# A recurrence and a two-layer block on one core: SyncE left out of the path for large h, and the last block's output turned by TensorE and stored in two transfers

## The chip, the cores and the metric

The kernel runs on 1 core of one Trainium2 chip. The metric is the time of one execution in device microseconds (us), the median over several runs. The span of a trace, from its first to its last instruction, is about 1.8 us shorter than the time of the same run.

In the views of the profile PE is TensorE, PEld its loading of weights, DVE VectorE, ACT ScalarE, POOL GpSimd and SP SyncE; a q behind the name is the engine's sequencer, the part that waits, branches and issues transfers, and L521 is line 521 of the kernel. A semaphore is a counter by which engines and transfers tell each other that they are done. An instruction fetch is a transfer that brings an engine its next instructions; the traces list these as packets of kind "instruction".

## The reference

```python
# attention part: B, S, D = 4, 6080, 256
sig = 1.0 / (1.0 + np.exp(-f_logit))
f = lower_bound + (1.0 - lower_bound) * sig
i = 1.0 - f
for t in range(S):
    h = f[:, t] * h + i[:, t] * x[:, t]
    y[:, t] = h
# second part, on all 24320 tokens: w_in 256 x 2048, w_out 2048 x 256
h = x @ w_in
g = h - np.tanh(h)
out = g @ w_out
```

The output is 24320 rows of 256 numbers in float32, 1 KB a row.

## The kernel before

The tokens are handled in 48 blocks: one of 256 and 47 of 512. A short polynomial stands for `h - tanh(h)` as long as all h are small. A flag watches that, and at the very end every engine reads the flag and branches: if some h was large, `general()` does all the work again with the real tanh. With these inputs that path is never run, but its code lies in the program, between the branch and the end.

In the main path a block's result stands in a tile `C` with channels on partitions. It has to be turned before it is stored with tokens as rows. VectorE turns it in squares of 32 x 32, which leaves rows of 64 numbers (256 B) on the partitions, and SyncE stores it with one transfer for each group of 32 partitions. The last block does this in four pieces and in two halves:

```python
def turn_out(j, slots=None):
    ...
    for slot in slots or (None,):
        ...
        nc.vector.transpose(out=dst[:, js, k], in_=src[:, js, k])

def send(j, half=None):
    ...
    dst = out[starts[j] : starts[j] + sizes[j], :].rearrange(
        "(j b) (i c) -> i b j c", b=H, i=G
    )
    for i in range(G):                      # G = 4: rows of 64 numbers
        nc.sync.dma_start(
            out=dst[i][:, js], in_=acc[j, "out"][i * H : (i + 1) * H, js])

def end(j):                                 # the last block alone
    ...
    for half, slot, r in ((0, 2, 1), (1, 1, 0)):
        nc.vector.tensor_tensor(
            out=C[:, slot], in0=acc[j, 3][:, r, 0:hb], in1=C[:, slot], op=ALU.add)
        turn_out(j, (slot,))
        send(j, half)
```

The last steps in the order of the program, and the branch:

```python
if (name, j) == ("o1", NBLK - 1):
    tc.mark_branch_hint_location("general", "LikelyTaken")
    nc.vector.reduce_max(out=worst[:], in_=flags[:], axis=mybir.AxisListType.X)
if j == NBLK - 1 and name in ("o4", "otr"):
    if name == "o4":
        sum_up()        # two tiny matmuls and a copy: worst -> flag
        end(j)
    continue
steps[name](j)
if (name, j) == ("o3", NBLK - 1):
    turn_out(j, (0, 3))
...
fast()
seen = nc.values_load(flag[:].bitcast(INT32), ...)   # on all five engines
with tc.If(seen != 0, label="general"):
    general()           # all its transfers are issued by nc.sync
```

## Time and profile before

| | before |
|---|---|
| median time | 2337.45 us (three runs, 2335.92 to 2338.53) |
| span of the trace | 2334.70 us |
| TensorE busy | 2318.4 us (99%) |
| start of the reduction of the flags to the end | 16.95 us |
| last arithmetic to the end | 11.45 us |

The prediction below shows the views that carry the argument. Two more are of use. First, who SyncE waited for at the end (engine and line waiting, what ended the wait, us in total, times, longest):

```profile
SPq L1006 <- SPq L1006: 2.4, 1, 2.4
```

A wait of an engine for its own branch is the time of a far jump, a branch over all of `general()` to the end: SyncE had nothing else to wait for. Second, the view of the output tile in the last 12.7 us (line, engine, operation, tiles and count; duration in ns as min/median/max; first and last start), with the time from issue to landing below it:

```profile
L521 SPq DMA_DIRECT2D out_dram<-osb x8: 315/450/2198, 2322.5 to 2329.3; - x8
...
DMA to landing us min/median/max: 1.9/3.6/3.8
```

Most issues take 0.45 us, but the longest took 2.2, and a store of 64 KB takes 1.9 us at best and 3.6 in the middle.

### The profile page before, as it was taken

The page shows a single profiled execution, that of the slowest core. Times are in us where ns is not written, and L with a number is a line of the kernel's source. Part 1 is how long each engine was busy: PE and PEld are TensorE (multiplying, and loading weights), DVE is VectorE, ACT ScalarE, POOL GpSimd, SP SyncE. Part 2 cuts the span into 40 slices and gives each one's busy share as a digit, 9 for nine tenths or more (in the row PEclk, how much of TensorE's full clock was granted, in tenths as well). Part 3 has the DMA queues.
Part 4 walks back from the last instruction along what each step waited for, and adds up shares of the span by engine and source line. Part 5 has one row for each costly group of instructions (what it writes and reads, how often), then busy time and mean ns, then how long its engine had stood idle before and what let it go on. Part 6 is the DMA issues. An engine that isn't in the chain of part 4 may idle for free.

```text
span 2334.7 us, 28635 instructions
## 1 busy us (share of the span) xinstructions
PE 2318.4 (99%) x10669; PEld 2024.6 (87%) x10669; DVE 2121.2 (91%) x2450; ACT 1800.4 (77%) x2685; POOL 0.7 (0%) x6
## 2 busy tenths in 40 slices
PE   9999999999999999999999999999999999999997
PEld 6888888888888888888888888888888888888886
DVE  8999899998999999998999989999899998999987
ACT  7677777777777777777777777777777777778774
POOL 0000000000000000000000000000000000000000
PEclk9999999999999999999999999999999999999999
DMA  5211111111111211112111121111211111111101
GB/s 172 63 23 35 39 37 28 28 39 35 37 28 28 45 29 37 28 28 46 31 34 28 28 46 36 28 28 30 44 37 28 28 36 37 37 28 28 28 10 29
DMA packets 298564, 85.05 MB, mean 36 GB/s; under 512 B 292016, under 2 KB 294320, under 8 KB 298416
## 3 DMA queue, kind: packets, MB, share of 16 engines
q1 hardware_dynamic: 298272, 83.14, 16.9%
q8 instruction: 85, 1.39, 0.3%
q14 instruction: 63, 0.52, 0.1%
q10 hardware_dynamic: 144, 0.00, 0.0%
HBM read 58.20 MB, written 24.90 MB: 36 GB/s over the span
## 4 chain that ended last, share of the span: by engine, by line
PE 99%; DMA 0%; SPq 0%; DVE 0%; issue 0%; DVEq 0%
PE A L383 27%; PE Qa L466 14%; PE Qb L466 14%; PE D L383 14%; PE Qd L466 14%; PE Qc L466 7%; PE B L383 7%; PE Qc L745 1%; PE Qa L745 1%; PE Qb L745 1%; PE A L678 1%; PE D L678 0%; PE Qd L678 0%; DMA xn<-in_x_dram 0%; PE B L678 0%; PE Qc L678 0%
## 5 line engine op out<-in xcount | busy, mean ns | idle before, releaser
L383 PE MATMUL A<-T,w_in 128*128 128x256 f32 x2208 | 558.8, 379 | 0.0
L383 PEld LDWEIGHTS A<-T,w_in 128*128 128x128 f32 x2208 | 419.5, 190 | 57.0
L427 DVE TENSOR_TENSOR h<-h,q 128x1024 f32<-128x1024 f32 x368 | 437.3, 1219 | 3.1
L421 DVE SCALAR_TENSOR_TENSOR q<-q,t 128x1024 f32<-128x1024 f32 x368 | 439.8, 1215 | 0.0
L414 ACT ACTIVATE q<-t 128x1024 f32<-128x1024 f32 x368 | 382.9, 1053 | 46.3 <-DVE h L427 43.4
L411 ACT ACTIVATE t<-h 128x1024 f32<-128x1024 f32 x368 | 388.6, 1056 | 3.1 <-DVE h L398 0.3
L432 ACT ACTIVATE junk<-t 128x1024 bf16<-128x1024 f32 x368 | 388.2, 1055 | 1.5
L446 DVE TENSOR_TENSOR Tg<-h 128x1024 f32<-128x1024 f32 x368 | 347.8, 945 | 6.3
L466 PE MATMUL Qb<-h,w_out 128*128 128x256 f32 x1472 | 347.7, 379 | 0.0
L466 PEld LDWEIGHTS Qb<-h,w_out 128*128 128x128 f32 x1472 | 279.7, 190 | 38.0
L466 PE MATMUL Qa<-Tg,w_out 128*128 128x256 f32 x736 | 219.0, 379 | 0.0
L466 PE MATMUL Qd<-Tg,w_out 128*128 128x256 f32 x736 | 218.9, 379 | 0.0
L466 PE MATMUL Qd<-h,w_out 128*128 128x256 f32 x736 | 218.9, 379 | 0.0
L466 PE MATMUL Qa<-h,w_out 128*128 128x256 f32 x736 | 218.9, 379 | 0.0
L395 ACT COPY h<-B 128x512 f32<-128x512 f32 x184 | 107.0, 581 | 143.3 <-PE B L383 94.5
L395 ACT COPY h<-A 128x512 f32<-128x512 f32 x184 | 107.2, 583 | 136.7 <-PE A L383 125.3
L398 DVE TENSOR_TENSOR h<-D,r 128x512 f32<-128x512 f32 x184 | 126.8, 689 | 93.6 <-PE D L383 91.3
L398 DVE TENSOR_TENSOR h<-A,r 128x512 f32<-128x512 f32 x184 | 126.2, 686 | 74.6 <-PE A L383 42.5
L395 ACT COPY r<-A 128x512 f32<-128x512 f32 x184 | 107.2, 583 | 106.0 <-PE A L383 106.0
L383 PE MATMUL B<-y,w_in 128*128 128x256 f32 x736 | 188.9, 379 | 0.0
L383 PE MATMUL D<-y,w_in 128*128 128x256 f32 x736 | 188.9, 379 | 0.0
L383 PE MATMUL A<-y,w_in 128*128 128x256 f32 x736 | 188.9, 379 | 0.0
(114 smaller groups left out, 3068.3 us busy)
## 6 DMA issues: line engine op xcount, KB each, us to landing
xn<-in_x_dram SPq DMA_DIRECT2D x184, 128.0 KB, 3.3
fn<-in_f_logit_dram SPq DMA_DIRECT2D x184, 128.0 KB, 3.2
out_dram<-osb SPq DMA_DIRECT2D x180, 128.0 KB, 2.8
raw<-in_moe_w_in_dram SPq DMA_DIRECT2D x8, 512.0 KB, 5.2
raw<-in_moe_w_out_dram SPq DMA_DIRECT2D x8, 512.0 KB, 4.7
fn<-in_f_logit_dram SPq DMA_DIRECT2D x1, 512.0 KB, 6.6
xn<-in_x_dram SPq DMA_DIRECT2D x1, 512.0 KB, 7.4
out_dram<-osb SPq DMA_DIRECT2D x1, 512.0 KB, 2.9
```

What stands on the lines that cost most here:

```text
L383: nc.tensor.matmul(ps[:, c], lhsT=w_in[u][:, slot, c * P : (c + 1) * P], rhs=mixes[j][right], start=start and c == 0, stop=True, skip_grou ...
L395: nc.scalar.copy(out=dst, in_=piece(n, bank))
L398: nc.vector.tensor_tensor(out=piece(n, "h")[:, q], in0=piece(n, bank), in1=piece(n, r), op=ALU.add)
L411: nc.scalar.activation(out=half(n, i, "t"), in_=half(n, i), func=AF.Square)
L414: nc.scalar.activation(out=half(n, i, "q"), in_=half(n, i, "t"), func=AF.Square, scale=RA, bias=RB,)
L421: nc.vector.scalar_tensor_tensor(out=q, in0=q, scalar=RC, in1=t, op0=ALU.add, op1=ALU.mult)
L427: nc.vector.tensor_tensor(out=h, in0=h, in1=q, op=ALU.mult)
L432: nc.scalar.activation(out=junk[:, :, :, 0 : st[n]["hb"]], in_=t, func=AF.Relu, bias=-TINY, accum_out=flags[:, 2 * n + i : 2 * n + i + 1],)
L446: nc.vector.tensor_tensor(out=o, in0=a, in1=b, op=ALU.subtract)
L466: nc.tensor.matmul(acc[j, part][:, r, 0 : st[n]["hb"]], lhsT=w_out[u][:, slot, c * P : (c + 1) * P], rhs=piece(n, right)[:, q, c], start=( ...
L678: nc.tensor.matmul(h[c], lhsT=w_in[u][:, 2 * k + s, c * P : (c + 1) * P], rhs=ys[j][:, k, 0:nb], start=k == 0 and (c == 0 or len(banks) == 2),
L745: nc.tensor.matmul(acc[j][i // 2][:, i % 2].rearrange("p (k m) -> p k m", k=2), lhsT=plain[j, u][:, s, c, i * P : (i + 1) * P], rhs=w_out[ ...
```

## The change

Two things are changed. The transfers of the path for large h are issued by GpSimd, so that SyncE has no code there to jump over. And the last block is turned by TensorE, 128 x 128 at a time, evicted by ScalarE (first half) and VectorE (second half), and stored in rows of 1 KB, one transfer of 256 KB for each half. Beside that, the flag is made earlier and a branch hint goes. The diff, cut to its core:

```diff
-        def fetch(j, parts=(0, 1)):
+        def fetch(j, parts=(0, 1), queue=nc.sync):
...
-                    nc.sync.dma_start(
+                    queue.dma_start(
...
         def end(j):
             hb = sizes[j] // 2
             C = acc[j, "C"][:, 0 : 4 * hb].rearrange("p (n t) -> p n t", n=4)
-            for half, slot, r in ((0, 2, 1), (1, 1, 0)):
+            osb = opool.tile([P, NQ, D], FP32, name="osb", tag="osb")
+            for half in range(2):
+                slot, r = ((2, 1), (1, 0))[half]
                 nc.vector.tensor_tensor(
                     out=C[:, slot], in0=acc[j, 3][:, r, 0:hb], in1=C[:, slot], op=ALU.add
                 )
-                turn_out(j, (slot,))
-                send(j, half)
+                name = ("Qa", "Qb")[half]
+                bank = ps_b.tile([P, 2, KC, P], FP32, name=name, tag=name)
+                for i in range(2):
+                    for k in range(KC):
+                        nc.tensor.transpose(
+                            bank[:, i, k], C[:, 2 * k + half, i * P : (i + 1) * P], ident[:]
+                        )
+                rows = osb[:, 2 * half : 2 * half + 2]
+                (nc.scalar.copy, nc.vector.tensor_copy)[half](
+                    out=rows.rearrange("p i (m k) -> p i k m", k=KC), in_=bank[:]
+                )
+                t0 = starts[j] + half * hb
+                nc.sync.dma_start(
+                    out=out[t0 : t0 + hb, :].rearrange("(i p) d -> p i d", p=P), in_=rows
+                )
...
-                            tc.mark_branch_hint_location("general", "LikelyTaken")
...
-                                sum_up()
                                 end(j)
                             continue
+                        if (name, j) == ("o3", NBLK - 1):
+                            sum_up()
                         steps[name](j)
-                        if (name, j) == ("o3", NBLK - 1):
-                            turn_out(j, (0, 3))
...     # in general(): weights, inputs and output
-                    fetch_w(u, raw[:], nc.sync)
+                    fetch_w(u, raw[:], nc.gpsimd)
-                fetch(j)
+                fetch(j, queue=nc.gpsimd)
-                nc.sync.dma_start(
+                nc.gpsimd.dma_start(
...
-    with tc.If(seen != 0, label="general"):
+    with tc.If(seen != 0):
```

More of the change, by code (lines that the diff above doesn't have):

```diff
@@ L498, in finish, with give @@
             nc.vector.tensor_tensor(out=o, in0=a, in1=b, op=ALU.add)
-        def turn_out(j, slots=None):
+        def give(j):
             n = sizes[j] // H
-            if (j, "out") not in acc:
-                acc[j, "out"] = opool.tile([P, TB // H, H * KC], FP32, name="osb", tag="osb")
-            dst = acc[j, "out"][:, 0:n].rearrange("p j (a k) -> p j k a", k=KC)
-            src = acc[j, "C"][:, 0 : n * KC * H].rearrange(
-                "p (k j b) -> p j k b", k=KC, b=H
-            )
-            for slot in slots or (None,):
-                k, s = (slice(None), 0) if slot is None else (slot // 2, slot % 2)
-                js = slice(0, n) if slot is None else slice(s * n // 2, (s + 1) * n // 2)
-                nc.vector.transpose(out=dst[:, js, k], in_=src[:, js, k])
-        def send(j, half=None):
-            n = sizes[j] // H
-            js = slice(0, n) if half is None else slice(half * n // 2, (half + 1) * n // 2)
+            osb = opool.tile([P, TB // H, H * KC], FP32, name="osb", tag="osb")
+            nc.vector.transpose(
+                out=osb[:, 0:n].rearrange("p j (a k) -> p j k a", k=KC),
+                in_=acc[j, "C"][:, 0 : n * KC * H].rearrange(
+                    "p (k j b) -> p j k b", k=KC, b=H
+                ),
+            )
             dst = out[starts[j] : starts[j] + sizes[j], :].rearrange(
@@ L521, in send @@
                 nc.sync.dma_start(
-                    out=dst[i][:, js],
-                    in_=acc[j, "out"][i * H : (i + 1) * H, js],
-                )
-        def give(j):
-            turn_out(j)
-            send(j)
+                    out=dst[i],
+                    in_=osb[i * H : (i + 1) * H, 0:n],
+                )
         def end(j):
```

## The prediction

> **What bounds the kernel now.** I read the page first (engines, then the chain that ended last), then the end of the chain in order of time, then the views of the three lines that come after the last arithmetic. The page of the kernel before, engines and chain:
>
> ```profile
> PE 2318.4 (99%) x10669; PEld 2024.6 (87%) x10669; DVE 2121.2 (91%) x2450; ACT 1800.4 (77%) x2685; POOL 0.7 (0%) x6
> ...
> PE 99%; DMA 0%; SPq 0%; DVE 0%; issue 0%; DVEq 0%
> ```
>
> TensorE is busy 2318.4 of 2334.7 us and the chain is TensorE: the body is bound by matmuls. The diff touches nothing in it (the stores of the 45 blocks before the last stay one VectorE transpose and four transfers each), so all it can win lies in the 16 us that TensorE is not busy, nearly all at the end. The chain of the last microseconds (start, length, what):
>
> ```profile
> 2318.92 0.88 PE Qc L466 x4
> 2319.80 0.02 issue
> 2319.82 0.43 DVE C L498
> ...
> 2320.89 0.77 DVE osb L512 x2
> 2321.66 0.33 DVE C L535
> 2321.99 0.02 issue
> 2322.01 0.45 DVE osb L512
> 2322.45 0.32 DVE C L535
> 2322.78 0.02 issue
> 2322.80 0.45 DVE osb L512
> ```
>
> Arithmetic ends at 2323.25, but the span at 2334.70: 11.45 us follow in which no engine computes. The timeline of SyncE (start, length) and the view of the line of the branch (duration ns, first and last start) say what they are:
>
> ```profile
> 2322.48 7.24 SPq L521 DMA_DIRECT2D out_dram<-osb  x8
> ```
>
> ```profile
> L1006 SPq EVENT_SEMAPHORE  x8: 17/17/17, 2332.8 to 2333.3; - x8
> ...
> L1006 POOLq COMPARE_BRANCH  x1: 45/45/45, 2322.4 to 2322.4; - x1
> L1006 PEldq COMPARE_BRANCH  x1: 4127/4127/4127, 2322.4 to 2322.4; - x1
> L1006 DVEq COMPARE_BRANCH  x1: 72/72/72, 2323.4 to 2323.4; - x1
> L1006 ACTq EVENT_SEMAPHORE  x1: 17/17/17, 2325.2 to 2325.2; - x1
> L1006 DVEq EVENT_SEMAPHORE  x1: 21/21/21, 2326.5 to 2326.5; - x1
> L1006 PEldq EVENT_SEMAPHORE  x1: 51/51/51, 2326.6 to 2326.6; - x1
> L1006 SPq COMPARE_BRANCH  x1: 45/45/45, 2330.3 to 2330.3; - x1
> ```
>
> SyncE is the last of all. From the single records (to the ns): eight issues 2322.48 to 2329.72 (six of 0.32 to 0.46 us, two of 2.20 and 2.14 us); read of the flag 2329.78 to 2330.27; branch at 2330.34; first instruction beyond it at 2332.82, **2.48 us** later; eight semaphore adds (0.59 us to the first wait of the end); eight waits and a drain to 2333.97; closing barrier to 2334.70 (**0.73 us**). The last packet of the output had ended at 2330.75, so no landing bounds this end: SyncE's own code does. GpSimd, which has no code in the path for large h, passes its branch and drains 0.16 us later (2322.40, 2322.56). Every engine with code there needs far more: ScalarE 2.85 us, VectorE 3.08, TensorE 4.18, SyncE 2.48. Each has an instruction page fetched 0.9 to 1.0 us after its branch. Both 2.2 us issues enclose a 16 KB instruction fetch of TensorE's (packets at 2323.47, 1.64 us, and 2327.31, 1.53 us); between the opening (its first 17 us) and the end there are ten more issues over 0.9 us, and all ten lie on such a fetch. So a store issued during TensorE's fetch is held about 2 us.
>
> **What the Trainium skill says.** (1) "Runtime: NRT & Kernel Launch", section Instruction fetch mechanics: a taken branch whose target isn't in the window held forces a fetch before execution can go on. The trace agrees: 2.5 to 4.2 us for the four engines that jump far, 0.16 us for the one that doesn't. (2) "DMA: Bandwidth & Descriptors", Specifications: line rate wants at least 512 B a descriptor; and Anatomy of one DMA: about 2 us are fixed, mostly the write receipt. The trace: rows of 256 B, 64 KB, took 3.6 us to land (median of eight); a store of 256 KB in rows of 1 KB took 2.2 us. Four times the data in less time agrees on both. (3) "VectorE: DVE Perf Modes", Why PSUM operands drop a tier: 1x only for fp32 from PSUM, so 512 columns at 0.96 GHz are 0.53 us plus overhead; the adds of 512 columns out of PSUM here took 0.69 us, which I use.
>
> **The change part by part.** *Flag earlier.* The two tiny matmuls for the flag go between Qc and Qd on TensorE. Before, they started 0.1 us behind the matmul rhythm and are 0.08 us loads: I put 0.2 us on Qd, whose end goes from 2321.51 to 2321.71. ScalarE copies the flag at about 2320.1 instead of 2321.67; this is off the path.
> *VectorE.* The four transposes of 256 columns (0.77 + 0.45 + 0.45 us of chain) go. The two adds (0.39 us each) start when Qd lands: 2321.8 to 2322.2 and 2322.2 to 2322.55. Before, the first waited for the transposes until 2321.58, so here little is won: the adds end 0.2 us earlier than 2322.77.
> *TensorE transposes.* In the opening the same operation has this record (min/median/max ns):
>
> ```profile
> L623 PE MATMUL Qb<-ident,fn x6: 283/283/417, 6.6 to 11.0; 128*128 128x128 f32 x6
> ```
>
> Two passes each, 0.12 us apart: 0.24 us a transpose. The first half's first needs no add and hides; three follow the add: 2322.25 to 2322.85, + 0.28 us of the last pass = 2323.13. The second half's four: last pass at 2323.81, end 2324.09.
> *Evictions.* ScalarE: 512 columns took 0.58 us (line 395), a start 0.1 us after the last pass: 2323.23 to 2323.82. VectorE: 2324.19 to 2324.88 (0.69).
> *Stores.* The same form of store stands in the opening:
>
> ```profile
> L762 SPq DMA_DIRECT2D out_dram<-osb x2: 400/402/404, 111.2 to 121.2; - x2
> ```
>
> Two issues of 0.40 us instead of eight: 2323.85 and 2324.9 to 2325.3. Landed 2.2 us after the issue starts, as its fastest did: 2327.1. SyncE then reads the flag (0.49 us), passes the branch as GpSimd did before (0.16 us) and waits for the landing; its eight adds go to GpSimd. A drain at about 2327.5. So **SyncE is 6.5 us earlier**, and it is no longer last.
> *The jump of the others.* Now the bound is the jump that starts last. TensorE reads the flag behind its last transpose, 2323.9; read and branch took 0.585 us (2321.856 to 2322.441), the jump 4.18, the drain 0.15: 2328.9. VectorE reads it when its eviction has started, 2324.2; + 0.62 + 3.08 + 0.11 = 2328.0. ScalarE 2323.25 + 0.53 + 2.85 + 0.09 = 2326.7. GpSimd now jumps too, but its flag comes at 2320.2; with TensorE's full 4.18 us and ten adds it is done by 2326.
> *Sum.* Last drain 2328.9 (TensorE), + 0.73 us barrier = 2329.65; before 2334.70. Gain **5.05 us**, 0.22%. The branch hint that goes is taken as worth nothing: with it, all four far jumps still fetched after their branch. GpSimd's transfers stand in the path not run: nothing in the body.
>
> **Rivals.** (a) *The second store is caught by TensorE's fetch.* Fetch at branch + 1.03 us = 2325.5; the issue ends by my sum at 2325.3, 0.2 us before. If it slips, it is held some 2 us: landing about 2328.9, drain 2329.2, end 2330.0. Costs only 0.3 us, since TensorE's jump is as long. For it: both issues that met such a fetch were held. About 1 in 3.
> (b) *The bound passes to GpSimd's or TensorE's jump, longer than measured*, as the hint is gone or as pages collide: GpSimd's jump has no record. 1 to 2 us more: 2333.5 to 2334.5. The early flag speaks against GpSimd.
> (c) *All is hidden*: were the output's landing the end, removing code would win nothing. Against it: the last packet ended 3.95 us before the end.
> (d) *A new cost in the body or the start* (other page borders, transfers on GpSimd's queue set up at the launch). I see nothing in the profile for it; at most a microsecond.
>
> **Range and chances.** 2337.45 - 5.05 = **2332.4 us**. The three runs before spread over 2335.92 to 2338.53, so the median alone is good to about 1.2 us; rivals (a) and (b) add up to 1.5 above, and shorter jumps up to 1 below. Range 2330.5 to 2334.6. 2% would be 47 us; the whole idle tail is 11.45 us, so neither more than 2% faster nor slower can come from here: 0.98 within 2%, 0.01 each way.
>
> **What would show it.** Right: SyncE's record at the branch is short and no adds follow it; two issues of 0.4 us in place of 7.24 us; the last to drain is TensorE, 4 us after a branch near 2324.5; the span is 2329 to 2331. Wrong: TensorE busy more than 0.2% longer in the body; a second store of over 2 us of issue (rival a); GpSimd last to drain (rival b); the span's end set by the landing; adds or far jump still on SyncE.

## The result, and the profile after

| | before | after |
|---|---|---|
| median time | 2336.56 us (six runs, 2335.92 to 2338.53) | 2331.41 us (six runs, 2330.55 to 2332.59) |
| span of the trace | 2334.70 us | 2329.32 us |
| start to the first product of the third block | 85.22 us | 85.49 us |
| from there to the reduction of the flags | 2232.54 us | 2232.54 us |
| reduction of the flags to the end | 16.95 us | 11.28 us |

The ratio of the times is 0.9977, with a 95% interval of 0.9964 to 0.999. A ratio is the mean time of one kernel's runs over that of the other's of the same rounds, so not quite the ratio of the medians quoted. The change is 5.2 us faster by the medians, and 5.38 us by the spans.

The last three rows cut the span in three. The middle is the same to 0.01 us in every trace, fourteen in all. The opening, where loads of inputs and weights meet, lasts from 85.2 to 87.4 us from trace to trace, whatever the kernel. That is most of the 2 us by which runs of one kernel differ, so the medians can't tell apart versions of the end that differ by a microsecond. The trace can: from here on, **"the end" is the time from the start of the reduction of the flags to the end of the span.** It is 5.67 us shorter after the change.

The chain that ended last, in the changed kernel (start, length, what; it follows arithmetic alone and stops at the last eviction):

```profile
2319.20 0.86 PE Qc L466 x4
2320.06 0.12 PE most L840 x2
2320.18 1.94 PE Qd L466 x8
...
2322.14 0.43 DVE C L526
...
2322.62 0.55 PE Qa L533 x3
2323.17 0.52 PE Qb L533 x4
...
2323.71 0.69 DVE osb L537
```

The arithmetic now ends 1.15 us later than before in the span, at 2324.40 in place of 2323.25 (0.28 us of that is the opening). The gain is not there. It lies behind it, in the view of the line of the branch:

```profile
L1009 POOLq EVENT_SEMAPHORE  x4: 17/43/43, 2324.0 to 2324.2; - x4
L1009 POOLq COMPARE_BRANCH  x1: 45/45/45, 2321.3 to 2321.3; - x1
L1009 PEldq COMPARE_BRANCH  x1: 3711/3711/3711, 2323.7 to 2323.7; - x1
...
L1009 DVEq COMPARE_BRANCH  x1: 72/72/72, 2324.3 to 2324.3; - x1
L1009 SPq COMPARE_BRANCH  x1: 50/50/50, 2325.6 to 2325.6; - x1
L1009 ACTq EVENT_SEMAPHORE  x1: 17/17/17, 2326.5 to 2326.5; - x1
L1009 PEldq EVENT_SEMAPHORE  x1: 51/51/51, 2327.4 to 2327.4; - x1
L1009 DVEq EVENT_SEMAPHORE  x1: 21/21/21, 2327.6 to 2327.6; - x1
```

SyncE branches at 2325.6 and no longer has semaphore adds behind its branch; its next instruction starts 0.19 us later. GpSimd has them instead, 2.7 us after its own branch at 2321.3. All jumps are over at 2327.6. Yet the span ends at 2329.32. What SyncE waits for, and how long the two stores take:

```profile
SPq L1039 <- DMA out_dram<-osb: 1.9, 2, 1.4
```

```profile
L541 SPq DMA_DIRECT2D out_dram<-osb x2: 389/389/389, 2323.8 to 2324.4; - x2
...
DMA to landing us min/median/max: 3.7/3.7/3.8
```

Two short issues replace the eight, but each store takes 3.7 us to land, and SyncE waits for that. The last landing is at 2328.18, SyncE drains at 2328.51, and the closing barrier takes 0.81 us. So **the landing of the last store sets the new end**, not a jump.

The single records say why it takes so long. A store runs on 16 DMA engines and each posts its own part of the semaphore; the Trainium skill ("DMA: Bandwidth & Descriptors", Why a DMA increments its semaphore by 16 and not by 1) describes this, and the trace has 16 updates for each store. For the second store, issued at 2324.43, eleven of the 16 arrive between 2326.54 and 2326.70, the next four by 2327.56, and the last at 2328.18. A packet of 16 KB, an instruction fetch of TensorE's after its branch, lies from 2324.71 to 2325.96, and smaller ones of 8 KB from 2324.60 on. The same page (Queues, rings and completion order) says that a DMA engine drains a whole packet of one queue before it turns to another. That fits: a part of the store that shares an engine with the fetch has to wait. It was an idea at this point; the experiments test it.

### The profile page after: what moved, and what is told of

The parts are those of the page before. It is cut to its first block, busy times and chain, and to the rows that moved or that the text cites. A ratio compares the mean times of both kernels' runs of the same rounds, so it can differ in the third digit from the quotient of the medians.

```text
span 2329.3 us, 28648 instructions
## 1 busy us (share of the span) xinstructions
PE 2319.6 (100%) x10677; PEld 2025.2 (87%) x10677; DVE 2121.4 (91%) x2447; ACT 1801.1 (77%) x2686; POOL 0.7 (0%) x6
## 4 chain that ended last, share of the span: by engine, by line
PE 99%; DMA 0%; SPq 0%; DVE 0%; issue 0%
PE A L383 27%; PE Qd L466 14%; PE Qa L466 14%; PE Qb L466 14%; PE D L383 14%; PE Qc L466 7%; PE B L383 7%; PE Qc L749 1%; PE Qb L749 1%; PE Qa L749 1%; PE A L682 1%; PE D L682 0%; PE Qd L682 0%; DMA xn<-in_x_dram 0%; PE B L682 0%; PE Qc L682 0%
```

## The experiments

My theory after the result: before the change, the end was SyncE's own code, that is eight issues of which two were held by TensorE's instruction fetch, then a jump of 2.5 us, then adds. The new end wins by getting its stores issued ahead of the fetch, and what is left of it is the landing of the last store, held by instruction fetches. The rivals: SyncE's jump is the whole gain; TensorE's transposes are the gain in themselves; two stores of 256 KB so close together need 3.7 us anyway; a branch costs the same, fetch or no fetch.

All of the runs gave right results on these inputs. The ends, in one table:

| run | what it is | the end, us | last store, issue to landing, us |
|---|---|---|---|
| before | | 16.95 | 1.9 |
| sp_free | before, SyncE out of the path for large h | 13.69 | 2.4 |
| no_branch_before | before, no path for large h at all | 11.06 | 1.9 |
| after | | 11.28 | 3.75 |
| after_again | the same | 12.02 | 4.49 |
| end_only | after, SyncE back in the path | 12.00 | 3.72 |
| eight_stores | after, eight stores of 64 KB | 15.69 | 1.7 |
| flag_late | after, flag made behind Qd | 10.73 and 10.76 | 3.5 |
| no_branch_after | after, no path for large h at all | 9.76 | 2.35 |
| near_jump | after, path for large h cut to some 20 to 40 instructions | 11.72 | 4.21 |
| near_jump_shift | the same, page border moved | 9.86 | 2.35 |
| pe_waits | after, TensorE's jump made 3.9 us later | 14.53 | 3.09 |
| pe_lingers | after, idle matmuls behind the transposes | 11.16 | 3.62 |

### SyncE's part alone

The end stays as before; `fetch`, `fetch_w` and the output of `general()` go to GpSimd:

```diff
 # before.py, general()
-                    fetch_w(u, raw[:], nc.sync)
+                    fetch_w(u, raw[:], nc.gpsimd)
...
-                fetch(j)
+                fetch(j, queue=nc.gpsimd)
...
-                nc.sync.dma_start(
+                nc.gpsimd.dma_start(
```

> The kernel before with one part of the change: the transfers of the path for large h are issued by GpSimd, the end is unchanged (VectorE transposes, eight stores of 64 KB). My theory, from the trace of before (span 2334.7 us): the eight issues still run until about 2329.7, two of them held 2 us each by TensorE's instruction fetch; then SyncE reads the flag and passes its branch in 0.2 us, so the jump of 2.5 us and the eight adds of 0.6 us go; now the last store's landing, 2331.1 in the trace of before, ends it: end = 2331.1 + 0.3 (last waits) + 0.75 (barrier) = 2332.2, that is 2.5 us less than before. Rival 1, SyncE's code is the whole of the change's gain: 5.4 us less. Rival 2, SyncE's code is hidden behind something else: 0.

Measured: the end went from 16.95 to 13.69 us, 3.26 less (ratio of the times 0.9992, interval 0.9978 to 1.0005, so the times alone don't show it). The jump and the adds are gone, and SyncE now waits for the landing:

```profile
SPq L1036 <- DMA out_dram<-osb: 0.2, 1, 0.2
```

It is 0.8 us more than my theory's 2.5, and the last issue ended 0.93 us earlier after the end of Qd: TensorE's two fetches were shorter in this trace (1.16 and 0.96 us in place of 1.64 and 1.53). The rival that asked for 5.4 us falls, and so does the one that asked for nothing.

### The new end alone

```diff
 # after.py, general(): all three back to nc.sync
-                    fetch_w(u, raw[:], nc.gpsimd)
+                    fetch_w(u, raw[:], nc.sync)
...
-                fetch(j, queue=nc.gpsimd)
+                fetch(j, queue=nc.sync)
...
-                nc.gpsimd.dma_start(
+                nc.sync.dma_start(
```

> The changed kernel with the other part undone: SyncE issues the transfers of the path for large h again, the end is the new one. My theory: the second issue ends at 2324.8 as in the changed kernel, flag read and branch at 2325.6, jump 2.5 us, adds 0.6, waits 0.55, barrier 0.75: end near 2330.0, 4.7 us less than before and 0.7 more than the changed kernel. The two parts alone would then sum to 7.2 us, more than the 5.4 of both together, as each shortens the same chain. Rival, the gains add: 5.4 - 2.5 = 2.9 us less than before.

Measured: 12.00 us, 4.95 less than before (ratio 0.998, 0.9967 to 0.9994). SyncE is back at its jump:

```profile
SPq L1009 <- SPq L1009: 2.5, 1, 2.5
```

The two parts alone sum to 3.26 + 4.95 = 8.2 us and together gave 5.67, as my theory said: they shorten the same chain. The new end is the larger part. Given the new end, taking SyncE out is worth 12.00 - 11.28 = 0.7 us against the first trace of the changed kernel and nothing against its second (12.02), as then the landing takes over.

### No branch at all

`values_load`, `tc.If` and `general()` are deleted from either kernel. These kernels are right for small h alone and serve as a measurement.

> The changed kernel without the path for large h and without its branch (right for these inputs alone). My theory: in the changed kernel the last store lands 3.7 us after its issue because one DMA engine carries TensorE's 16 KB instruction fetch first (15 of the 16 engines had posted within 3.1 us, eleven within 2.3); without a jump there is no fetch, the second store lands 2.2 us after its issue, near 2326.6, and the span ends near 2327.7: 1.6 us less than the changed kernel, 7.0 less than before. Rival, two stores of 256 KB so close together need 3.7 us anyway: landing 2328.2 and the span 2329.0 to 2329.3.

> The kernel before without the path for large h and without its branch (right for these inputs alone). My theory: no issue is held any more, eight issues of 0.45 us take 3.7 instead of 7.2 us, 2322.5 to 2326.2; last landing near 2327.5, span near 2328.6: 6.1 us less than before, and only 0.9 us above the changed end without a branch. So nearly all that the new end wins, it wins by getting its stores issued ahead of TensorE's fetch. Rival, the new end is itself much faster (transposes, wide rows): 2332 or more, 4 us above no_branch_after.

Measured for the changed kernel: 9.76 us. All 16 parts of the last store post within 0.20 us, and it lands 2.35 us after its issue. The view of the output tile:

```profile
DMA to landing us min/median/max: 2.2/2.3/2.3
```

So two stores of 256 KB that close together need 2.3 us, not 3.7; that rival falls. For the kernel before, 11.06 us, and no issue is held:

```profile
L521 SPq DMA_DIRECT2D out_dram<-osb x8: 316/459/467, 2323.7 to 2327.1; - x8
```

Without a branch the new end is 11.06 - 9.76 = 1.3 us better than the old one (I had put 0.9). With the branch and SyncE free it is 13.69 - 11.28 = 2.4 us better, or 1.7 against the second trace. So once SyncE is free, at most 1.1 us of what the new end wins, less than half, can come from its two issues being ahead of the fetch; the other 1.3 us are there without any fetch. My "nearly all" was wrong there. It fits better with SyncE in the path of both, where each hold of an issue also delays SyncE's jump: of 16.95 - 12.00 = 4.95 us only 1.3 are there without a fetch. The trace of before has the fetch 1.96 us after the end of Qd, and the third of eight issues ran into it; in the changed kernel the second and last issue began 0.28 us before the fetch and was not held (0.39 us). The times of both show no more than the medians allow (0.9977 and 0.9981).

### Jump or fetch

The path for large h is cut to one quarter of one block, so that the target of the branch is near. The kernel would be wrong for large h.

```diff
 # after.py, general()
-            for u in range(NU):                    # weights
+            for u in range(1):
...
-            for j, nb in enumerate(sizes):
+            for j, nb in enumerate(sizes[:1]):
...
-                for u in range(NU):                # products
+                for u in range(1):
...
```

> The changed kernel with the path for large h cut down to one quarter of one block, some 20 to 40 instructions an engine in place of 709 to 4,629 (it would be wrong for large h, which these inputs never have; the branch, the flag and the end stay). Measured in the trace from the start of the reduction of the flags to the end of the span: before 16.95 us, changed 11.28, changed without the branch 9.76. My theory, it is the far jump's instruction fetch that costs, not the branch: no 16 KB fetch after the branch, TensorE drains within 0.5 us of its branch, the last store lands 2.3 to 2.5 us after its issue, 9.8 to 10.1 us. Rival, a taken branch costs the same near or far: 11.3.

Measured: 11.72 us, which neither side had. TensorE's branch is short:

```profile
L1009 PEldq COMPARE_BRANCH  x1: 367/367/367, 2325.3 to 2325.3; - x1
```

but the stores are slower than ever:

```profile
DMA to landing us min/median/max: 4.2/4.2/4.2
```

The records show the cause: one 16 KB packet of TensorE's queue still came, 1.1 us after its branch, and it took 1.73 us. Fifteen parts of the last store posted within 0.17 us, the sixteenth 1.9 us after them. In the traces TensorE's fetches come 218 to 288 of its records apart, 256 on average (without the first of a trace and those behind the branch), so I take one fetch to bring a page of some 256 instructions (an estimate from these distances). The last fetch before this one was 274 records earlier: the program happened to reach a page border just at its end. So I moved the border, by 60 tiny matmuls at the start, where TensorE waits for data:

```diff
 # near_jump
+            for _ in range(60):
+                nc.tensor.matmul(
+                    busy[:, 0:8], lhsT=zeros.bitcast(BF16)[:, 0:P],
+                    rhs=zeros.bitcast(BF16)[:, 0:8], start=True, stop=True,
+                    skip_group_check=True,
+                )
             open_by(before.split())
```

> In near_jump no engine took more than 0.43 us over its branch, yet one 16 KB fetch of TensorE's came 1.1 us after it (its instructions reach a page border just there) and one of 16 engines posted the last store 1.9 us after the other 15. This run is near_jump with 60 tiny matmuls (120 records) at the very start, while TensorE waits for its data anyway, so that the page border is crossed earlier and none lies at the end. My theory, the fetch alone holds the landing: no 16 KB fetch after the last block's matmuls, all 16 engines post within 0.3 us, the last store lands 2.3 to 2.5 us after its issue, 9.7 to 10.1 us from the reduction of the flags to the end (near_jump 11.72, without the branch 9.76). Rival, the branch or the flag reads slow the store in another way: 11 or more again.

Measured: 9.86 us, with the branch, the flag reads and the path still there. No fetch lies at the end. The view of the output tile:

```profile
DMA to landing us min/median/max: 2.2/2.3/2.3
```

That is the same end as without a branch, to 0.1 us. Between the ends of these two runs nothing differs but where the page border falls, and they differ by 1.86 us. This shows that a single fetch of 16 KB holds one sixteenth of the last store, and with it the end. The ends are of one trace each, but the times agree: five runs of 2331.45 to 2333.17 us with the fetch and four of 2329.86 to 2331.36 without, each set on its own chip (before took 2337.55 and 2337.20 us there).

One thing stays open. In the changed kernel too TensorE had come to such a border, 272 records after its last fetch, when it branched. No run moves the border with the far jump in place, so it is not shown that the far jump would bring this fetch away from a border; that the fetch holds the store is.

### TensorE's fetch made late

The first attempt put ten idle matmuls (2.2 us) behind the transposes.

> The changed kernel with ten idle bf16 matmuls (2.2 us) on TensorE after its last transposes, so that its flag read, branch and 16 KB fetch come 2.2 us later, after the stores have gone. My theory: with TensorE's fetch out of the way the last store lands at most 2.8 us after its issue (3.75 in the changed kernel); the end is then set by TensorE's own late jump, 12.4 us from the reduction of the flags to the end. Rival, the 8 KB fetches of ScalarE and VectorE hold the store: it still lands over 3.4 us after its issue.

It missed: the flag was read 1.00 us after the end of Qd, as ever (0.96). TensorE's sequencer handed the matmuls over and went on to the branch before they ran, and the store landed in 3.6 us. The run tells nothing of the cause. The second attempt makes TensorE wait for a semaphore, by a last matmul on a tile that ScalarE fills five times:

```diff
 # after.py, end(), second half
+                    late = tpool.tile([P, TB], FP32, name="t", tag="t")
+                    for _ in range(5):
+                        nc.scalar.copy(out=late[:], in_=zeros[:])
+                    spare = ps_b.tile([P, TB], FP32, name="B", tag="B")
+                    nc.tensor.matmul(spare[:], lhsT=late[:].bitcast(BF16)[:, 0:P], ...)
```

> The test that pe_lingers missed (there the sequencer ran ahead of the idle matmuls and branched when it always did). Here the last matmul waits for five idle copies on ScalarE, so that TensorE's and ScalarE's flag reads, far jumps and fetches come about 3 us later, after the stores have gone; VectorE's 8 KB fetch stays where it was. My theory: the last store lands at most 2.9 us after its issue (3.75 in the changed kernel) though every jump is still there; the end is then TensorE's late jump, 13.5 to 14.5 us from the reduction of the flags to the end. Rival, the two stores or the 8 KB fetch of VectorE are what holds: over 3.4 us after its issue.

Measured: the fetch came at 6.48 us after the end of Qd in place of 2.61, and the view of the output tile reads:

```profile
DMA to landing us min/median/max: 2.5/2.8/3.1
```

The last store landed 3.09 us after its issue, in between: 0.2 over my theory's bound and 0.3 below the rival's. Fifteen of its parts were there 2.34 us after the issue, as without a branch, and one came 0.75 us later. No 16 KB fetch was left near the store, only fetches of 8 KB. So by elimination these hold a part too, for less; no run takes them away alone. TensorE's accounts for the rest (3.75 - 3.09 = 0.66 us here, 1.9 in near_jump). Which of the 8 KB fetches it was, GpSimd's or VectorE's, I did not separate. The end, 14.53 us, is TensorE's late jump, just above my 13.5 to 14.5.

### Wide rows or TensorE's transposes

```diff
 # after.py, end()
-                nc.sync.dma_start(
-                    out=out[t0 : t0 + hb, :].rearrange("(i p) d -> p i d", p=P), in_=rows
-                )
+                dst = out[t0 : t0 + hb, :].rearrange("(i p) d -> p i d", p=P)
+                for c in range(4):
+                    nc.sync.dma_start(
+                        out=dst[:, :, c * 64 : (c + 1) * 64],
+                        in_=rows[:, :, c * 64 : (c + 1) * 64],
+                    )
```

> The changed kernel with each half stored by four transfers of 64 KB in rows of 256 B, as before, out of the same tile turned by TensorE. My theory: the number of issues is what counts; the third or so is held by TensorE's fetch to about 4.0 us after the end of Qd, the last ends near 6.3 and lands near 7.7, the span ends 1.5 to 2.2 us later than the changed kernel: 12.8 to 13.5 us from the reduction of the flags to the end. Rival, the transposes by TensorE and the early eviction are the gain: 11.3 to 11.6.

Measured: 15.69 us (ratio of the times to before 0.9997, interval 0.9982 to 1.0012), 4.4 more than the changed kernel and 2.0 more than sp_free, which stores the same eight pieces out of VectorE's transposes. Two issues were held 2.1 and 1.9 us:

```profile
L543 SPq DMA_DIRECT2D out_dram<-osb x8: 388/489/2117, 2323.7 to 2330.6; - x8
```

My theory had the right sign but only 1.5 to 2.2 us: I reckoned one long hold and a small second one. The rival falls clearly. TensorE's transposes win nothing by themselves; the first store is issued 1.74 us after the end of Qd with them and 0.97 with VectorE's. They are the price of rows of 1 KB, and **the two wide stores are the gain**. Whether it is their number or the width of their rows, no run separates. The record points to the number: where no fetch came, a store of 64 KB in rows of 256 B landed in 1.7 to 1.9 us and one of 256 KB in rows of 1 KB in 2.2 to 2.35, so narrow rows were not slow to land, but the eight issues took 3.9 us (no_branch_before) and the two 1.0 (no_branch_after).

### The early flag

```diff
 # after.py
+                                sum_up()          # at o4, before end(j)
                                 end(j)
-                        if (name, j) == ("o3", NBLK - 1):
-                            sum_up()
```

> The changed kernel with the flag's two matmuls and copy back behind Qd, as before. My theory: the early flag serves GpSimd's jump alone, which has slack: GpSimd drains near 4.2 us after the end of Qd in place of 2.4, TensorE's and SyncE's ends stay; 11.2 to 11.4 us from the reduction of the flags to the end. Rival, the early flag is a part of the gain: 12 or more.

Measured: 10.73 us, below my range. GpSimd drains 4.11 us after the end of Qd in place of 2.41, without harm, as I expected, but Qd ends 0.32 us earlier, as the two flag matmuls stand in front of it in the changed kernel. As that kernel would be right for all inputs, I timed it beside the changed one.

> The changed kernel once more, unaltered, to see how well the end repeats. From the reduction of the flags to the end: 11.28 us in its first trace. My theory, the end depends on how long the fetches take on the way (1.1 to 1.3 us for TensorE's), so 10.9 to 11.6 us; the whole time 5 us below before, with the opening's jitter of some 2 us on top. Rival, the end does not repeat to half a microsecond and the small differences between the experiments mean nothing.

> flag_late, timed beside the changed kernel, as its one trace ended 0.55 us sooner (10.73 us from the reduction of the flags to the end; 0.33 us of it lies before the end of Qd, where the flag's matmuls stand in the changed kernel). My theory: 10.6 to 11.1 us in the trace, 0.3 to 0.5 us less than the changed kernel; that is too little for the medians, whose runs spread over 2 us. Rival, nothing repeats of it: the same as the changed kernel within 0.1 us in the trace.

Measured: 12.02 us for the changed kernel (median 2333.35, ratio 0.9983) and 10.76 for flag_late (median 2332.34, ratio 0.9979). The end of flag_late repeats to 0.03 us. That of the changed kernel does not: TensorE's fetch came 1.92 us after its branch in place of 1.06,

```profile
L1009 PEldq COMPARE_BRANCH  x1: 4627/4627/4627, 2325.3 to 2325.3; - x1
```

and the stores landed later still:

```profile
DMA to landing us min/median/max: 4.4/4.4/4.5
```

So my range for the changed kernel was wrong, and differences under 0.7 us between ends that contain a fetch mean little. In both traces flag_late's end was the shorter, by 0.6 and 1.3 us, and by 0.4 against pe_lingers, which is nearly a third trace of the changed kernel (11.16 us); only the 0.32 us before the end of Qd are explained. Whether the rest (GpSimd's own fetches coming at another moment) is a cause or chance stays open with two traces each. The medians, 1.0 us apart, don't resolve it.

No run takes the branch hint away alone. The trace of the kernel before has no record of a hint instruction, and TensorE's jump took 3.7 and 4.2 us in the two traces with the hint and 3.6 to 4.7 in those without, so nothing is seen of it.

## Why the prediction was right

The forecast was 2332.4 us and a span gain of 5.05; the runs gave 2331.41 and 5.38. Step by step, with times from the start of the reduction of the flags so that the opening drops out (the forecast's times less 2317.76, the measured ones less 2318.03):

| step | forecast, us | measured, us |
|---|---|---|
| Qd ends | 3.95 | 4.07 |
| both adds done | 4.79 | 4.87 |
| last transpose done | 6.33 | 5.64 |
| first store issued | 6.09 | 5.81 |
| second store issued | 7.14 | 6.40 |
| last store landed | 9.34 | 10.15 |
| SyncE drained | 9.74 | 10.47 |
| TensorE's branch | 6.74 | 5.62 |
| TensorE drained | 11.14 | 9.54 |
| VectorE drained | 10.24 | 9.66 |
| GpSimd drained | 8.2 | 6.49 |
| the end | 11.89 | 11.28 |

**What held.** The bound of before was read rightly: sp_free and end_only together show that SyncE's issues, jump and adds were the chain. SyncE's record at the branch became short, no adds follow, two issues of 0.39 us took the place of 7.24 us. GpSimd's new jump had slack. The body did not change by 0.01 us. Nothing was seen of the hint. Rival (a) did not come: the second issue began 0.28 us before TensorE's fetch and was not held.

**What did not, though the sum came out.** Three terms were off, and they partly cancelled.

First, "two passes each, 0.12 us apart: 0.24 us a transpose" was a misreading. The group it was taken from has six records for six transposes, two of a block of 256 tokens and four of a block of 512, so one pass each. After the change:

```profile
L533 PE MATMUL Qb<-ident,C x4: 272/272/300, 2323.0 to 2323.4; 128*128 128x128 f32 x4
```

Four records for four transposes, 0.11 us apart. The Trainium skill ("TensorE: Matmul & The Clock Gate", Part 4: PE-mode transpose) gives about 275 ns for one in a kernel's context, beside a figure for bf16 in isolation; here it is float32, and the record has 272. With this the last transpose was done 0.7 us before the forecast. TensorE's branch came 1.1 us before it, as its flag was not read behind the last transpose but began 0.34 us before that one started. The jump was 0.4 us shorter than in the trace of before (3.77 us in place of 4.18), for which the forecast had left room only in its range. The forecast's sum for TensorE also slips by 0.1: 2323.9 + 0.585 + 4.18 + 0.15 is 2328.8, which gives a gain of 5.15.

Second, "landed 2.2 us after the issue starts, as its fastest did" was mis-sized: 3.75. I had taken it from the opening, where one store of this size stands. I had seen that TensorE's fetch holds issues, and as rival (a) I asked whether the second issue would meet it, but held that an issue which ended in time was safe. It isn't: the packets are moved 0.9 us after the issue begins and one DMA engine is then busy with the fetch. The runs show 2.35 us with no fetch (near_jump_shift, no_branch_after), and 3.75, 4.49 and 4.21 with one. The same oversight is in the forecast's point (2): "four times the data in less time agrees on both" set 3.6 us for narrow rows beside 2.2 for wide ones, but the 3.6 was the fetches' doing. In no_branch_before the same narrow stores landed in 1.7 to 1.9 us, so the two numbers say nothing about the width of rows.

Third, and as a result of both, the last to drain was SyncE, waiting for the landing, and not TensorE. The forecast listed that as a sign of a wrong step ("the span's end set by the landing"), and it was one. TensorE drained at 9.54 us in place of 11.14, SyncE at 10.47 in place of 9.74, so the last drain, and with it the end, came 0.6 to 0.7 us before the forecast. That the sum came so near is in part luck: a path too long by 1.6 us and a landing too short by 0.8 lay on two sides of it, and the second trace of the same kernel, with the fetch later, ended at 12.02, 0.1 us after the forecast.

## What to carry to other kernels

In a program with a large piece of code that is skipped at the end, look at the time between the last arithmetic and the end of the span: every engine that had code in the skipped piece paid a far jump (2.5 to 4.7 us here), and TensorE's instruction fetch held a part of the store in flight. Take engines that issue the last stores out of that piece (3.3 us here with the old end, 0 to 0.7 with the new one), and send the last result in few, wide transfers issued before the others branch, even at the price of a dearer transpose. When the change is worth less than the jitter of the opening, measure the stretch that it touches in the trace, from a fixed instruction to the end, and take a second trace before you read anything into half a microsecond.

## What the Trainium skill lacked or had wrong

- "Runtime: NRT & Kernel Launch", Instruction fetch mechanics: it says that a far jump stalls its engine but not for how long, nor what the fetch does to others. Here the stall was 2.5 to 3.4 us (SyncE, ScalarE, VectorE, GpSimd), and 3.6 to 4.7 for TensorE; cut to a near jump, 0.2 to 0.4 us.
- The same section calls the cost of crossing a page "mostly hidden". Near the end it was not: one sequential 16 KB fetch cost 1.86 us of the span (near_jump against near_jump_shift). It also gives 16 KiB as the unit of refill; here TensorE's queue had 16 KB packets (85 in the span), and the queue of the others 8 KB ones.
- "DMA: Bandwidth & Descriptors", Queues, rings and completion order: that instruction fetches delay parts of a kernel's store, the last by 0.75 to 2.1 us, stands nowhere; nor that SyncE's issue of a transfer is itself held meanwhile. The hold has no fixed length: all twelve issues over 0.9 us that lie on a 16 KB fetch in the trace of before (0.9 to 2.2 us long) ended 0.39 to 0.43 us after the fetch did.
- No page says that TensorE's sequencer passes a branch while matmuls handed over earlier still wait to run; pe_lingers shows it, with its flag read 2.7 us before its last matmul ended (1.00 and 3.72 us after the end of Qd).
